# Early loads of a one-core SSM and linear-attention kernel: decay vectors at the head of GpSimd's queue, x in pairs ahead of B

## The chip, the cores and the metric

One core of one Trainium2 chip. The metric is the device time of one execution of the whole program in microseconds. The core has five engines with a queue each: TensorE (PE: matrix products, with weight loads PEld beside them), VectorE (DVE), ScalarE (ACT), GpSimd (POOL) and SyncE (SP), which here only issues DMAs.

## The reference, cut to what matters

The input x has 2048 rows of 512. Two branches read it, and a gate per row mixes them.

```python
g = sigmoid((x * gate_w).sum(-1, keepdims=True))
# a: diagonal state space model
Lam_bar = exp(exp(log_dt) * (Lambda_re + 1j * Lambda_im))
Bu = einsum("bld,pd->blp", x, ((Lam_bar - 1) / Lam)[:, None] * Bmat)
h_t = Lam_bar * h_(t-1) + Bu_t                      # 2048 steps
a = 2 * real(einsum("blp,dp->bld", h, Cmat)) + x * Dskip
# b: linear attention, 32 heads of 16
q, k, v = x @ wqkv
phi = concat(softmax(.. @ w_phi), softmax(-(.. @ w_phi)))   # of q and of k
b = (phi_q @ (phi_k^T v)) / (phi_q . sum phi_k + 1e-6) @ wo
out = g * a + (1 - g) * b
```

## The kernel before, in words

The rows of x are put into 16 tiles of 128 (tile `ti` holds every eighth row: residue `ti // 2`, half `ti % 2`), and each tile is loaded transposed, so that its 512 features lie along the partitions: `x_load(ti)`, a transposing DMA issued by SyncE into a slice of `xT` (L230). All products that read x use these tiles.

The work is cut into some 250 small generators (`st_...`), and a string `ORDER` written out by hand (L24 to L53) says in which order their steps are recorded. A token names a generator, and each time it stands there the generator goes one step on: the first step of `k3@5` records the four products of K for tile 3 into PSUM bank 5, the second `k3` records the cast that empties the bank. `:D` or `:A` picks VectorE or ScalarE for such a cast; `F:28` records 28 filler products that compute nothing. Each engine works through its own instructions strictly in the recorded order and waits on semaphores where another engine's or a DMA's result is needed. The hardware DMAs of SyncE and ScalarE share eight completion semaphores (lanes) in turn, and an issue waits until the transfer that used its lane before has landed.

The stages, in the order of TensorE:

- Fold: `W0..W3` transpose the K weights (`ptw`, L275), `f0..f3` multiply them with BD, a block diagonal of `w_phi` (`pf`, L432), and casts write `Wk2`. BD (L344) needs `mask16`, which VectorE reduces from an identity matrix that GpSimd makes (`make_identity`); the identity is also what TensorE transposes with.
- The three decay vectors go into `vec_n` by three small GpSimd DMAs (L252), `V` transposes them on TensorE (`pvt`, L311), and `P`, `P2`, `P3`, `P4`, `U`, `i0..i3` and `M` work out decay factors and tables on ScalarE, VectorE and GpSimd.
- `k0..k15` and `v0..v15` are the products of K and V of the 16 tiles (L476, names `pk` and `pv`). `x`, `n`, `e`, `s` make the softmax features of groups of tiles on VectorE and ScalarE (`EEk`; the last step, L549, scales them), and `a0..a4` sum features times V into `kvacc` (L579).
- `g..` are the products with B (`pgq`, L602), fed by `NR` and `NI`, which load both halves of B (`Bn`, L285), and `R0..R7`, which transpose it by DMA (L289). Later come the scan (`z`, `h`), the queries (`q`), and the outputs (`y`, `o`, `t`).

SyncE's queue before the change: `w_phi`, x tiles 0 to 3, the V weights `Wv` (L239), x tiles 4 to 7, then from `ORDER` both halves of B, seven of the x tiles 8 to 15 one by one (`l10 l13 l9 l12 l14 l11 l8`), `R0`, `R1`, `l15`, and further transposes.

Of the kernel before, what the change touches and what calls it, by code (L numbers as in the profile page):

```python
# [23 lines left out]
ORDER = """  # L24
NR F:28 NI B W1@0 W0@1 W0 W2@2 W1:D W3@3 W3 f1@4 W2:D f0@5 f2@6 f0 f1:D l10 V@0 F:4 V P f3@1 f3 f2:D F:4 P P k1@2 k1
l13 P2 k0@3 P2 U P2 P2 P2 P2 P4 k2@4 P3 P3 k3@5 P4 P4 k0 v0@0 i0 i2 U i0 i0 i1 i2 k4@7 i0:D i0 k2 i2 i2:D i2 U k3 k5@6
i1 v3@1 n0 x0 l9 i1 V2@2 i3 l12 x0 k4 v2@3 i3 i3 l14 i1 k5 n0 x0 n0 x0 i3 k7@4 n0 x0 U n0 i1 l11 k6@5 n1 x1 x1 n1 x1
n1 l8 R0 R1 x1 i3 k7 M v7@7 x1 n1 n1 k6:D L V2 v1@6 x2 n2 e0 v6@4 v5@5 v4@2 e0 x2 s0 v0 l15 n2 s0 n2 v2 s0 v1 R2 s0 v6
v3 n2 k10@0 k10 s0 k9@3 k9 C4 k13@6 gw D R3 s0 k12@4 e1 v7 s0 e1 s1 C6 k11@1 k11 x2 s1 k14@0 k8@3 k12 k14 k8 v4 k13
a0@71 a0 x2 s1 x2 s1 v5 g00@4 g00 g60@0 n2 x3 s1 g20@3 g60 s1 g10@2 g10 n3 e2 g30@6 g40@5 g10 s1 a1 x3 g20 n3 a1 x3 n3  # L30
x3 g41@4 n3 C3 e2 e2 e2 x3 g30 g40 g30 k15@0 k15 n3 e3 s2 x4 s2 x4 g01@2 g01 e3 e3 s2 g50@3 g11@5 g50 s2 s2 s2 n4 x4
n4 Q3 n4 s2 g50 g21@6 e3 s3 v8@0 g31@2 g11 Q2 g11 n4 g70@3 Q1 s3 C7 g21 g70 v9@5 g70 g70 z0 z0 g31 g31 Q0 w1@6 C0 a2
a2 a2 w0@3 s3 z0 v11@2 v9 g61@5 g41 R4 z0 w1 v8 z0 z0 g61 s3 w2@4 s3 s3 a2 x4 z0 z0 g51@6 g51 x4 w2 C2 s3 w3@0 g51 v11
n4 R5 w3 g71@5 g71 g71 g71 z1 z1 g02@4 g02 g42@6 a3 a3 z0 z0 g42 w0 e4 e4 z1 z1 z1 g62@2 g12@0 q1@5 C1 h50@4 C5 J1 e4
e4 z1 q2@6 q2 g12 g12 g22@3 g22 J0 h50 z1 z1 g62 q3@4 q3 J2 s4 z1 s4 q0@6 z1 s4 q0 q1 xA nA g32@0 J3 g32 g32 h60@3 J0
g52@2 g52 c4 h60 J2 c4 g52 h51@4 c2 s4 s4 g72@6 R7 g72 xA h10@5 nA g72 g72 c2 xA J3 nA h10 v10@0 v10 J1 s4 c5 h51 c5
R6 g23@3 v12@2 c4 c0 c0 g63@5 nA z2 z2 a3 a3 g03@4 xA g03 z2 z2 z2 z2 xA g23 z2 z2 g33@6 c5 v12 z2 z2 g13@0 g13 g63
g43@4 h32@3 g13 nA g43 h52@2 h52 g33 h32 h61@5 h61 h12@0 c0 g53@4 h12 g33 g53 s4 v14@3 c2 eA eA h42@2 h42 g73@6 g53 eA
eA g73 g73 q10@5 sA h11@0 h11 O h00@4 g73 sA v13@2 h00 v13 a4 z3 sA v15@6 z3 v15 h20@0 h01@4 h30@2 v14 h20 sA h30 z3
h31@6 z3 z3 sA a4 h01 h31 c6 c6 sA q13@3 q13 z3 a4 a4 Y Y h22@0 G q10 z3 z3 G q6@2 q6 h22 z3 z3 sA sA Y Y c1 c1 q9@4  # L40
q8@6 q5@7 h62@3 h41@5 c3 h41 c1 c3 c3 h13@0 h62 q11@2 h13 q11 q8 q12@1 c6 q12 h21@5 q5 h21 h02@2 c7 q4@6 q4 h53@3 h53
h23@1 h23 h33@0 h33 sA q9 h40@7 h40 sA q7@5 h43@6 h63@3 c7 h43 q7 c7 y4@0 y4 sA h63 sA h03@1 END h02 o0@4 o0 X1 N1
o1@7 o1 q14@6 X1 N1 h03 o0@5 X1 o1@2 o1 o1 o0 o0 q15@3 o2@4 o2 o2@7 o2 N1 q15 X1 N1 X1 N1 E1 E1 y2@1 y1@2 y1 E1 E1 q14
X2 y0@5 y0 o1 y4 X2 N2 X2 o0 o0 o3@4 o3 o3@7 o3 o1 o3 y2 X2 N2 o2 X2 N2 S1 S1 N2 S1 o3 S1 N2 S1 S1 o3 y5@3 o2 o2 S1 S1
S1 y1 E2 E2 E2 E2 y9@6 G N3 y5 y5 y3@4 y2 X3 X3 N3 t1 G t1 N3 S1 N3 S2 y9 y9 S2 S2 S1 S1 S2 y3 y3 t3 y0 t0 t0 t2 t2
y6@7 X3 t2:A o4@2 o4 o4@5 o4 o4 y6 y6 t3 X3 o4 X3 o4 S2 S2 t3 o5@1 o5 o5@2 o5 o5 y13@5 y13 o5 N3 o6@4 S2 o6 o6@1 o6 o6
y12@2 o5 y7@4 y7 y12 o6 o6 t4 y7 S2 S2 t4:D S2 E3 E3 E3 E3 S2 o7@1 o7 t5 t5 S3 o7@0 o7 S3 o7 t6 S3 o7 S2 o7 y8@1 o8@3
t6 o8 o8@0 o8 o8 S3 S3 y12 t0:A y11@7 o8 o8 o9@3 o9:D o9@0 o9:D S3 y8 y8 o9 o9 S3 S3 o9 o10@3 y11 o10 o10@0 y11 o10
o10 S3 y14@3 S3 y14 t7 t7:D t8 y14 t8 y15@0 o11@4 S3 o11 o11@1 t9 o12@4 o11:D o11 S3 o10 o10 o12 o12@1 o12 o12 t9:D
o11 y15 o13@4 o13:D o13@6 t6:A o13 o13 o11 o12 y10@1 o14@4 y15 o14:D o12@6 t9 o12:D t7:A t1 y10 y10 o13 o15@4 o15  # L50
o15@6 t4:A t5 o15 o15 t8 o15 t12 t12 t12:A t10 o14@4 o14 o14 t10:D o13@6 t11 o15@2 o15 t10 o13:D t11 t11:A y13 t13 o14
o14@1 t15 t13 t13 t15 t15 o14:D t14 t14 t14:A
"""  # L53
# [16 lines left out]
def kernel(  # L70
# [156 lines left out]
    x_res = x2.rearrange("(a c r) d -> r a c d", r=NR, c=P)

    def x_load(ti):
        nc.sync.dma_start_transpose(out=xT[:, :, ti * P:(ti + 1) * P], in_=x_res[ti // 2, ti % 2])  # L230
# [8 lines left out]
    nc.sync.dma_start(out=Wv[:], in_=B_wqkv[:, 2 * D:3 * D].rearrange("(k p) n -> p k n", p=P))  # L239
# [7 lines left out]
    tabp = tab_g.__enter__()  # L247
    iot = tabp.tile([P, NC], F32, name="iot", bufs=1)
    nc.gpsimd.iota(iot[:], pattern=[[1, NC]], base=0, channel_multiplier=0, allow_small_or_imprecise_dtypes=True)
    for t_, srcs in ((vec_n, (A_Lambda_im, A_Lambda_re, A_log_dt)), (vec_m, (A_Dskip, gate_w))):  # L250
        for n, src in enumerate(srcs):
            nc.gpsimd.dma_start(out=t_[4 * n:4 * n + 4, :], in_=src.rearrange("(j p) -> j p", p=P))  # L252
# [608 lines left out]
```

## Time and profile before

| | us |
|---|---|
| three runs | 155.34, 154.69, 155.97 (median 155.34) |
| the profiled execution | 155.2 |
| its span in the profile | 153.1 |
| TensorE busy | 147.5 (96%) |
| VectorE busy | 133.1 (87%) |
| ScalarE busy | 129.3 (84%) |
| GpSimd busy | 15.8 (10%) |
| mean granted clock of TensorE | 0.998 |

The span runs from the first to the last instruction of the program; the execution's own time is 2.1 us longer. In a row of the timeline the first number is the start, the second the length, then engine, line, operation, output<-inputs, and `x20` for twenty merged instructions; brackets hold the idle time before it and what ended it. `SPq` is the issue of a DMA, whose data lands later. A busy TensorE in these rows is not TensorE at its peak, since its products overlap: the distance from one start to the next tells the rate.

### The profile page before, as it was taken

The page shows a single profiled execution, that of the slowest core. Times are in us where ns is not written, and L with a number is a line of the kernel's source. Part 1 is how long each engine was busy: PE and PEld are TensorE (multiplying, and loading weights), DVE is VectorE, ACT ScalarE, POOL GpSimd, SP SyncE. Part 2 cuts the span into 40 slices and gives each one's busy share as a digit, 9 for nine tenths or more (in the row PEclk, how much of TensorE's full clock was granted, in tenths as well). Part 3 has the DMA queues.
Part 4 walks back from the last instruction along what each step waited for, and adds up shares of the span by engine and source line. Part 5 has one row for each costly group of instructions (what it writes and reads, how often), then busy time and mean ns, then how long its engine had stood idle before and what let it go on. Part 6 is the DMA issues. An engine that isn't in the chain of part 4 may idle for free.

```text
span 153.1 us, 3382 instructions
## 1 busy us (share of the span) xinstructions
PE 147.5 (96%) x1254; PEld 95.5 (62%) x1254; DVE 133.1 (87%) x304; ACT 129.3 (84%) x279; POOL 15.8 (10%) x43
## 2 busy tenths in 40 slices
PE   7999979999999999999999999999999999999990
PEld 7844434788878986869867656555555555546550
DVE  3799999999999999999999999999999858716441
ACT  3589998999998999999998999699488998618471
POOL 8239980000000000000000000000000000000000
PEclk9999999999999999999999999999999999999999
DMA  4785996494455699720000007911159959989943
GB/s 122 158 215 77 232 160 143 99 79 104 103 107 100 133 222 178 167 97 4 0 0 4 0 0 167 76 37 33 36 98 144 178 125 187 168 139 186 255 145 104
DMA packets 50992, 17.55 MB, mean 115 GB/s; under 512 B 44192, under 2 KB 50976, under 8 KB 50976
## 3 DMA queue, kind: packets, MB, share of 16 engines
q1 hardware_dynamic: 49120, 15.82, 57.0%
q10 hardware_dynamic: 1696, 1.51, 3.1%
q8 instruction: 10, 0.16, 0.5%
q0 software_dynamic: 160, 0.01, 0.2%
q14 instruction: 6, 0.05, 0.2%
HBM read 2.64 MB, written 2.10 MB: 31 GB/s over the span
## 4 chain that ended last, share of the span: by engine, by line
PE 80%; SPq 9%; DMA 8%; issue 1%; DVE 0%; ACT 0%
PE pgq L602 18%; PE py L718 16%; PE py L766 9%; PE pq L476 9%; SPq L230 7%; DMA xT<-in_A_x_dram 5%; PE pk L476 5%; PE pv L476 5%; PE ph L669 4%; DMA phT<-EEq 3%; PE kvacc L579 3%; PE pn L737 3%; PE pgq L607 2%; PE py L723 2%; PE pgq L609 2%; SPq L285 1%
## 5 line engine op out<-in xcount | busy, mean ns | idle before, releaser
L602 PE MATMUL pgq<-xT,BT 128*128 128x256 bf16 x256 | 31.5, 273 | 0.0
L476 PEld LDWEIGHTS <-xT 128*128 128x128 bf16 x192 | 18.1, 97 | 19.2 <-DMA xT<-in_A_x_dram 1.7
L602 PEld LDWEIGHTS <-BT 128*128 128x128 bf16 x256 | 24.6, 98 | 4.1
L139 ACT ACTIVATE EEk<-EEk 128x1024 bf16<-128x1024 bf16 x20 | 20.5, 1082 | 0.0
L120 ACT CAST uv<-pgq 128x512 bf16<-128x512 f32 x28 | 15.9, 605 | 0.7 <-PE pgq L602 0.5
L766 PE MATMUL py<-Wo,oT 128*128 128x512 bf16 x64 | 15.9, 380 | 0.0
L476 PE MATMUL pv<-Wv,xT 128*128 128x512 bf16 x64 | 15.8, 379 | 0.0
L476 PE MATMUL pq<-Wq,xT 128*128 128x512 bf16 x64 | 15.6, 379 | 0.0
L476 PE MATMUL pk<-Wk,xT 128*128 128x512 bf16 x64 | 14.8, 380 | 0.8 <-DMA xT<-in_A_x_dram 0.8
L139 ACT ACTIVATE EEq<-EEq 128x1024 bf16<-128x1024 bf16 x12 | 11.7, 1043 | 0.2 <-DVE EEq L528 0.2
L139 ACT ACTIVATE ld<-pn 128x16 f32<-128x16 f32 x32 | 6.1, 191 | 6.1 <-PE pn L737 4.7
L778 ACT ACTIVATE ot<-py,G 128x512 bf16<-128x512 f32 x11 | 7.4, 689 | 4.0 <-PE py L766 3.6
L591 ACT ACTIVATE phT<-X,dgB 128x512 bf16<-128x512 bf16 x16 | 10.7, 725 | 0.0
L120 ACT CAST nu<-pn 128x256 bf16<-128x256 f32 x27 | 9.9, 381 | 0.0
L745 DVE TENSOR_TENSOR on<-nu,rd 128x512 bf16<-128x512 bf16 x16 | 6.7, 421 | 3.5 <-ACT rd L139 1.8
L120 ACT CAST Xq<-pk 128x512 bf16<-128x512 f32 x15 | 8.6, 597 | 1.3 <-PE pk L476 1.3
L120 ACT CAST vx<-pv 128x512 bf16<-128x512 f32 x16 | 9.1, 603 | 0.4 <-PE pv L476 0.4
L549 DVE TENSOR_TENSOR EEk<-EEk,rck 128x4096 bf16<-128x4096 bf16 (+1 forms) x5 | 9.3, 1859 | 0.0
L120 ACT CAST Xq<-pq 128x512 bf16<-128x512 f32 x16 | 8.9, 609 | 0.2 <-PE pq L476 0.2
L766 PEld LDWEIGHTS <-oT 128*128 128x128 bf16 x64 | 5.5, 97 | 5.7 <-DMA oT<-on 0.8
L737 PEld LDWEIGHTS <-phT 128*128 128x128 bf16 x128 | 6.3, 97 | 3.5 <-DMA phT<-EEq 0.8
L512 DVE TENSOR_TENSOR smk<-smk 128x512 bf16<-128x512 bf16 (+4 forms) x18 | 8.1, 447 | 0.1
(180 smaller groups left out, 323.9 us busy)
## 6 DMA issues: line engine op xcount, KB each, us to landing
X<-HM SPq DMA_DIRECT2D x8, 256.0 KB, 4.4
out_dram<-ot SPq DMA_DIRECT2D x8, 128.0 KB, 2.2
out_dram<-ot ACTq DMA_DIRECT2D x7, 128.0 KB, 2.7
C2r<-in_B_wqkv_dram ACTq DMA_DIRECT2D x2, 256.0 KB, 3.5
Wv<-in_B_wqkv_dram SPq DMA_DIRECT2D x1, 512.0 KB, 4.1
Bn<-in_A_B_re_dram SPq DMA_DIRECT2D x1, 512.0 KB, 6.4
Bn<-in_A_B_im_dram SPq DMA_DIRECT2D x1, 512.0 KB, 7.2
Wo<-in_B_wo_dram SPq DMA_DIRECT2D x1, 512.0 KB, 4.1
```

What stands on the lines that cost most here:

```text
L120: nc.scalar.copy(out=out_ap, in_=in_ap)
L139: ins = nc.scalar.activation(**kw)
L230: nc.sync.dma_start_transpose(out=xT[:, :, ti * P:(ti + 1) * P], in_=x_res[ti // 2, ti % 2])
L476: MM(out=pt[:], lhsT=xT[:, kt, ti * P:(ti + 1) * P], rhs=W[:, kt, :], start=(kt == 0), stop=(kt == KT - 1))
L512: VT(out=dst, in0=cur[:, :, :, 0:n, :], in1=cur[:, :, :, n:2 * n, :], op=op)
L549: VT(out=E5, in0=E5, in1=rc.to_broadcast([P, L, 2 * NB, Dh, 4]), op=ALU.mult)
L591: nc.scalar.mul(out=t_, in_=x_, mul=c_)
L602: MM(out=pg[:, h, :], lhsT=BT[:, kt, 2 * j + h, :], rhs=xT[:, kt, r * NC:(r + 1) * NC], start=(h == 0 and kt == 0), stop=(r % 2 == 0 and k ...
L718: MM(out=py[:], lhsT=hs(r, t, slice(a * P, (a + 1) * P)), rhs=C2B[t], start=(t == 0), stop=False)
L737: MM(out=pn[:, 4 * m:4 * m + 4, :].rearrange("p h e -> p (h e)"), lhsT=ph[:, 4 * hf + m, :], rhs=KVm[:, 4 * hf + m, :], start=(m == 0), st ...
L766: MM(out=py[:], lhsT=oT[:, g, :], rhs=Wo[:, g, :], start=False, stop=(g == HG - 1))
L778: nc.scalar.mul(out=ot[:], in_=py[:], mul=G[:, ti:ti + 1])
```

## The change

Four things move; what is computed stays.

- The three GpSimd DMAs of the decay vectors are issued ahead of `make_identity`; those of Dskip and the gate stay behind it.
- `V` stands between the folds `f1` and `f0` instead of behind all but one; there are 34 fillers instead of 36.
- x tiles 0 and 1 are loaded singly, then `Wv`, then pairs of tiles in one transposing DMA each: 2-3, 4-5, 6-7 and 10-11, then both halves of B, then 8-9, 12-13, 14-15, and only then the transposes of B. Before, four single tiles stood ahead of `Wv`, four behind it, and eight behind B.
- The order of products begins `k0 k1 v0 k2 k3 k4 k5` instead of `k1 k0 k2 k3 v0 k4 k5`; the second half goes `k10 k11 k9 k12 k13 k14 k8` instead of `k10 k9 k13 k12 k11 k14 k8`.

```diff
-NR F:28 NI B W1@0 W0@1 W0 W2@2 W1:D W3@3 W3 f1@4 W2:D f0@5 f2@6 f0 f1:D l10 V@0 F:4 V P f3@1 f3 f2:D F:4 P P k1@2 k1
-l13 P2 k0@3 P2 U P2 P2 P2 P2 P4 k2@4 P3 P3 k3@5 P4 P4 k0 v0@0 i0 i2 U i0 i0 i1 i2 k4@7 i0:D i0 k2 i2 i2:D i2 U k3 k5@6
+l10 NR NI l8 l12 l14 F:28 B W1@0 W0@1 W0 W2@2 W1:D W3@3 W3 f1@4 W2:D V@0 f0@5 f2@6 V P f0 f1:D f3@1 P f3 F:6 f2:D P P2
+k0@2 P2 k0 P2 U k1@3 P2 P2 P2 P4 v0@0 k2@4 P3 P3 k3@5 P4 P4 k1 i0 i2 U i0 i0 i1 i2 k4@7 i0:D i0 k2 i2 i2:D i2 U k3
...
-    x_res = x2.rearrange("(a c r) d -> r a c d", r=NR, c=P)
-    def x_load(ti):
-        nc.sync.dma_start_transpose(out=xT[:, :, ti * P:(ti + 1) * P], in_=x_res[ti // 2, ti % 2])
+    x_res = x2.rearrange("(ac r) d -> r ac d", r=NR)
+    def x_load(ti, n=2):
+        a = ti % 2
+        nc.sync.dma_start_transpose(out=xT[:, :, ti * P:(ti + n) * P], in_=x_res[ti // 2, a * P:(a + n) * P])
+    def rows_in(t_, srcs):
+        for n, src in enumerate(srcs):
+            last_row = nc.gpsimd.dma_start(out=t_[4 * n:4 * n + 4, :], in_=src.rearrange("(j p) -> j p", p=P))
+        return last_row
+    rows_in(vec_n, (A_Lambda_im, A_Lambda_re, A_log_dt))
     make_identity(nc, ident[:])
...
-    for ti in range(4):
-        x_load(ti)
+    for ti in range(2):
+        x_load(ti, 1)
     nc.sync.dma_start(out=Wv[:], in_=B_wqkv[:, 2 * D:3 * D].rearrange("(k p) n -> p k n", p=P))
-    for ti in range(4, 8):
+    x_load(2)
+    for ti in (4, 6):
         x_load(ti)
...
-    for t_, srcs in ((vec_n, (A_Lambda_im, A_Lambda_re, A_log_dt)), (vec_m, (A_Dskip, gate_w))):
-        for n, src in enumerate(srcs):
-            nc.gpsimd.dma_start(out=t_[4 * n:4 * n + 4, :], in_=src.rearrange("(j p) -> j p", p=P))
+    rows_in(vec_m, (A_Dskip, gate_w))
```

More of the change, by code (lines that the diff above doesn't have):

```diff
@@ L30 @@
[L30 to L44, printed above, removed]
@@ new lines @@
+e3 s3 v8@0 g31@2 g11 Q2 g11 n4 g70@3 Q1 s3 C7 g21 g70 v9@5 g70 g70 z0 z0 g31 g31 Q0 w1@6 C0 a2 a2 a2 w0@3 s3 z0 v11@2
+v9 g61@5 g41 R4 z0 w1 v8 z0 z0 g61 s3 w2@4 s3 s3 a2 x4 z0 z0 g51@6 g51 x4 w2 C2 s3 w3@0 g51 v11 n4 R5 w3 g71@5 g71 g71
+g71 z1 z1 g02@4 g02 g42@6 a3 a3 z0 z0 g42 w0 e4 e4 z1 z1 z1 g62@2 g12@0 q1@5 C1 h50@4 C5 J1 e4 e4 z1 q2@6 q2 g12 g12
+g22@3 g22 J0 h50 z1 z1 g62 q3@4 q3 J2 s4 z1 s4 q0@6 z1 s4 q0 q1 xA nA g32@0 J3 g32 g32 h60@3 J0 g52@2 g52 c4 h60 J2 c4
+g52 h51@4 c2 s4 s4 g72@6 R7 g72 xA h10@5 nA g72 g72 c2 xA J3 nA h10 v10@0 v10 J1 s4 c5 h51 c5 R6 g23@3 v12@2 c4 c0 c0
@@ new lines @@
+g63@5 nA z2 z2 a3 a3 g03@4 xA g03 z2 z2 z2 z2 xA g23 z2 z2 g33@6 c5 v12 z2 z2 g13@0 g13 g63 g43@4 h32@3 g13 nA g43
+h52@2 h52 g33 h32 h61@5 h61 h12@0 c0 g53@4 h12 g33 g53 s4 v14@3 c2 eA eA h42@2 h42 g73@6 g53 eA eA g73 g73 q10@5 sA
+h11@0 h11 O h00@4 g73 sA v13@2 h00 v13 a4 z3 sA v15@6 z3 v15 h20@0 h01@4 h30@2 v14 h20 sA h30 z3 h31@6 z3 z3 sA a4 h01
+h31 c6 c6 sA q13@3 q13 z3 a4 a4 Y Y h22@0 G q10 z3 z3 G q6@2 q6 h22 z3 z3 sA sA Y Y c1 c1 q9@4 q8@6 q5@7 h62@3 h41@5
+c3 h41 c1 c3 c3 h13@0 h62 q11@2 h13 q11 q8 q12@1 c6 q12 h21@5 q5 h21 h02@2 c7 q4@6 q4 h53@3 h53 h23@1 h23 h33@0 h33 sA
@@ new lines @@
+q9 h40@7 h40 sA q7@5 h43@6 h63@3 c7 h43 q7 c7 y4@0 y4 sA h63 sA h03@1 END h02 o0@4 o0 X1 N1 o1@7 o1 q14@6 X1 N1 h03
+o0@5 X1 o1@2 o1 o1 o0 o0 q15@3 o2@4 o2 o2@7 o2 N1 q15 X1 N1 X1 N1 E1 E1 y2@1 y1@2 y1 E1 E1 q14 X2 y0@5 y0 o1 y4 X2 N2
+X2 o0 o0 o3@4 o3 o3@7 o3 o1 o3 y2 X2 N2 o2 X2 N2 S1 S1 N2 S1 o3 S1 N2 S1 S1 o3 y5@3 o2 o2 S1 S1 S1 y1 E2 E2 E2 E2 y9@6
+G N3 y5 y5 y3@4 y2 X3 X3 N3 t1 G t1 N3 S1 N3 S2 y9 y9 S2 S2 S1 S1 S2 y3 y3 t3 y0 t0 t0 t2 t2 y6@7 X3 t2:A o4@2 o4 o4@5
+o4 o4 y6 y6 t3 X3 o4 X3 o4 S2 S2 t3 o5@1 o5 o5@2 o5 o5 y13@5 y13 o5 N3 o6@4 S2 o6 o6@1 o6 o6 y12@2 o5 y7@4 y7 y12 o6
@@ new lines @@
+o6 t4 y7 S2 S2 t4:D S2 E3 E3 E3 E3 S2 o7@1 o7 t5 t5 S3 o7@0 o7 S3 o7 t6 S3 o7 S2 o7 y8@1 o8@3 t6 o8 o8@0 o8 o8 S3 S3
+y12 t0:A y11@7 o8 o8 o9@3 o9:D o9@0 o9:D S3 y8 y8 o9 o9 S3 S3 o9 o10@3 y11 o10 o10@0 y11 o10 o10 S3 y14@3 S3 y14 t7
+t7:D t8 y14 t8 y15@0 o11@4 S3 o11 o11@1 t9 o12@4 o11:D o11 S3 o10 o10 o12 o12@1 o12 o12 t9:D o11 y15 o13@4 o13:D o13@6
+t6:A o13 o13 o11 o12 y10@1 o14@4 y15 o14:D o12@6 t9 o12:D t7:A t1 y10 y10 o13 o15@4 o15 o15@6 t4:A t5 o15 o15 t8 o15
+t12 t12 t12:A t10 o14@4 o14 o14 t10:D o13@6 t11 o15@2 o15 t10 o13:D t11 t11:A y13 t13 o14 o14@1 t15 t13 t13 t15 t15
@@ L53 @@
+o14:D t14 t14 t14:A
 """
```

16 lines of the change are left out of this document (5 added, 11 removed).

## The prediction

> **What bounds the kernel now.** I read the page first, then the busy time by stretches, then the chain of waits, then TensorE's timeline around the one place where the chain leaves TensorE.
>
> ```profile
> span 153.1 us, 3382 instructions
> PE 147.5 (96%) x1254; PEld 95.5 (62%) x1254; DVE 133.1 (87%) x304; ACT 129.3 (84%) x279; POOL 15.8 (10%) x43
> ```
>
> ```profile
> 22.00:30.00 8.00, 7.64 (x59) 4.06 (x60) 7.93 (x19) 7.14 (x15) 0.51 (x1) 1.00 0.64 131
> 30.00:45.00 15.00, 15.00 (x148) 12.62 (x147) 14.93 (x26) 14.97 (x27) 0.00 (x0) 1.00 0.62 98
> 45.00:60.00 15.00, 15.00 (x184) 12.30 (x183) 14.91 (x32) 14.30 (x29) 0.00 (x0) 1.00 0.84 159
> ```
>
> The columns of the second view are the stretch, its length, then the busy time of TensorE, its weight loads, VectorE, ScalarE and GpSimd, the granted clock and DMA. VectorE is full from 22 us on (7.93 of 8, then 14.9 of 15), TensorE from 30 us; between 22 and 30 us TensorE alone has a hole. Where both are full, time given to one of them alone is worth only what the other can follow.
>
> ```profile
> 14.42 7.89 DMA xT<-in_A_x_dram
> ...
> 57.12 0.86 PE pq L476 x4
> ```
>
> ```profile
> 17.06 4.49 PE L476 MATMUL pv<-Wv,xT 128*128 128x512 bf16 x20
> 22.36 6.34 PE L476 MATMUL pk<-Wk,xT 128*128 128x512 bf16 x28 [0.80 <-DMA xT<-in_A_x_dram]
> 28.54 0.42 PE L579 MATMUL kvacc<-vx,EEk 128*128 128x68 bf16 x8
> ...
> 34.71 0.42 PE L579 MATMUL kvacc<-vx,EEk 128*128 128x68 bf16 x8
> ```
>
> The chain of waits shows one transfer of x, issued at 14.42 us and landing 7.89 us later at 22.31; TensorE goes on 0.05 us behind it. Unstalled, four 512-column products take 0.86 us (0.215 each). Twenty from 17.06 would end at 21.36, and the next starts at 22.36: a stall of 1.0 us. The 28 products from 22.36 should take 6.02 us, and the following group starts 6.18 us later, so 0.15 us more is lost, again to x. That is the whole early stall: 1.15 us.
>
> **What the change does, part by part.**
>
> **x in pairs, ahead of B.** SyncE issues these one after the other:
>
> ```profile
> 1.31 5.21 SPq L230 DMA_TRANSPOSE xT<-in_A_x_dram  x4
> 6.57 0.59 SPq L239 DMA_DIRECT2D Wv<-in_B_wqkv_dram  x1
> ...
> 12.37 1.34 SPq L285 DMA_DIRECT2D Bn<-in_A_B_re_dram  x1
> 13.75 0.62 SPq L285 DMA_DIRECT2D Bn<-in_A_B_im_dram  x1
> ```
>
> A single tile costs 5.21/4 = 1.3 us of the queue. A pair moves twice the data; no such transfer of x is in the trace. The nearest row is the transpose into phT, [128, 8, 128] against [128, 4, 128] for a tile of x, so just as much data as a pair (its source is SBUF, not HBM):
>
> ```profile
> L564 SPq DMA_TRANSPOSE phT<-EEq x12: 1247/1292/2247, 113.1 to 138.7; - x12
> ```
>
> Its median issue, 1.29 us, is that of half the data. I take 1.3 us for a pair; the upper end is twice a tile, 2.6, the lower the 1.25 us of phT's fastest. With 1.3 the queue runs: tiles 0 and 1 at 1.31 and 2.65, Wv at 3.94, pair 2-3 at 4.58, 4-5 at 5.9, 6-7 at 7.2, 10-11 at 8.5, the two halves of B at 9.8 and 11.1, then 8-9 at 11.8, 12-13 at 13.1, 14-15 at 14.4. The lane waits before these issues are for transfers landed by then. Seven issues fewer take some 9 us off the queue, and the first transpose of B goes out when B has landed, by 19.0 us if its second half takes the 7.89 us of the tile behind it today; the last tiles of x no longer stand in front of it.
>
> [...]
>
> Landing, from issue, by the page's last column:
>
> ```profile
> Wv<-in_B_wqkv_dram SPq DMA_DIRECT2D x1, 512.0 KB, 4.1
> ...
> xT<-in_A_x_dram SPq DMA_TRANSPOSE x16, 3.9
> oT<-on SPq DMA_TRANSPOSE x12, 2.7
> phT<-EEq SPq DMA_TRANSPOSE x12, 3.3
> ```
>
> So Wv lands at 8.0. A tile of x takes 3.9 us, and a pair adds the 0.6 us by which phT, twice the data, takes longer than oT: pair 2-3, issued at 4.58, lands at 9.1. The far bound is the tile behind B, 7.89 us, hence 12.5. The order of products becomes k0, k1, v0, k2: with 0.86 us a tile from 7.4, k2 starts at 10.0. It is met by 0.9 us. Pair 4-5, 1.3 us behind, has until 11.7; 6-7 until 15. Tile 10 is wanted at 21.4 and tile 9 at 23.1, both over 3 us behind their landing even with B's 7 us counted. The 1.15 us stall goes: **-1.15 us** on TensorE.
>
> V of tile 0 ahead of k2 is a change of order among equal products (0.86 each): nothing by itself. It gives pair 2-3 that time, and if Wv were later than 9.1 it would cost what it is late.
>
> **Vectors first on GpSimd.** Three issues now stand ahead of the identity, which VectorE needs for the mask of the fold operand BD.
>
> ```profile
> 0.79 0.20 POOL masks.py:197 MEMSET ident<- 128x128 bf16 x1 [0.29 <-POOLq L845]
> ...
> 1.42 0.28 POOL masks.py:199 TENSOR_SCALAR_AFFINE_SELECT identf<-identf 128x128 f32<-128x128 f32 x1
> ...
> 1.96 0.77 POOL L252 DMA_DIRECT2D vec_n<-in_A_Lambda_im_dram  x1
> 2.74 0.52 POOL L252 DMA_DIRECT2D vec_n<-in_A_Lambda_re_dram  x1
> 3.26 0.52 POOL L252 DMA_DIRECT2D vec_n<-in_A_log_dt_dram  x1
> ```
>
> ```profile
> 2.75 0.06 DVE L257 MEMSET eps_p<- 64x1 f32 x1
> 4.06 0.69 DVE L344 TENSOR_TENSOR BD<-Wc,mask 128x512 bf16<-128x512 bf16 x1 [1.25 <-DMA Wc<-in_B_w_phi_dram]
> 4.90 0.42 DVE L122 COPY Xq<-ptw 128x512 bf16<-128x512 bf16 x1
> ```
>
> They take 0.77 + 0.52 + 0.52 = 1.81 us, so the float identity is done at 1.70 + 1.81 = 3.51. Behind it on VectorE stand the two reductions, maskN and the eps memsets, which end 1.11 us after it today (2.81): now 4.62. BD follows at 4.65 instead of 4.06, and the copy of W1 behind it ends at 4.65 + 0.69 + 0.42 = 5.76 or a little more. The first fold starts today at 5.78:
>
> ```profile
> 5.78 0.85 PE L432 MATMUL pf<-BD,Xq 128*128 128x128 bf16 x12
> 6.56 0.18 PE L311 MATMUL pvt<-ident,vec_n 12*128 12x12 bf16 x1
> ```
>
> With 0.05 us from an end to TensorE's start it goes at 5.83 to 5.87: **+0.05 to +0.09 us**. The cover is the 1.25 us that BD now waits for Wc, and the wait of W1's copy for its transposes. BD later than about 4.6 costs one for one. The bound upward is all three issues at 0.77: BD at 5.15, +0.55.
>
> **V between the folds.** V ran at 6.56, so the vectors had landed by then; issued 1.17 us earlier (0.79 against 1.96) they land by 5.4, before f1 ends at about 6.05. V (0.18) now stands ahead of f0, f2 and f3 on TensorE, its cast ahead of f1's on VectorE, the exponential ahead of f0's cast on ScalarE.
>
> ```profile
> 7.01 0.21 ACT L139 ACTIVATE ssm_par<-vec 128x4 f32<-128x4 f32 x1
> ```
>
> The same small instructions run as before, and two filler products fewer; what follows on VectorE starts about 0.09 us late at most, and k0 at 7.4 instead of 7.35. I put this inside the +0.09. Its bounds are -0.14 (two fillers saved, 0.07 each as the fold's products, 0.85 for 12) and +0.21 (the exponential, put in front of a cast that k0 needs).
>
> **Where the stall goes.** TensorE comes 1.06 us earlier to the first sums of K and V, at 27.5 instead of 28.54. They read the features that VectorE finishes here:
>
> ```profile
> 26.68 1.22 DVE L549 TENSOR_TENSOR EEk<-EEk,rck 128x2048 bf16<-128x2048 bf16 x1
> ...
> 33.03 1.22 DVE L549 TENSOR_TENSOR EEk<-EEk,rck 128x2048 bf16<-128x2048 bf16 x1
> ```
>
> VectorE is full up to there, and nothing in its work is taken away. It ends the first group at 27.90, the second at 34.25. TensorE waits at the first until 27.96 (0.58 of the gain is left), and at the second until 34.31 against 34.71: 0.40 is left, less VectorE's own 0.09. Behind that both run in step to 115 us, so what is left reaches the end.
>
> **The sum:** -1.15 + 0.09 + 0.48 (wait at the first sums) + 0.27 (at the second) = **-0.3 us**. The profiled execution took 155.2 us, 2.1 outside its span; that gives 154.9. The median of the three runs is 155.34, which gives 155.0. I forecast **155.0**: 0.2% less.
>
> **The rivals.**
>
> *VectorE follows.* If the work of VectorE also moved up, the full 1.06 to 1.15 would stay: 154.1. For it: x and the vectors are earlier. Against: VectorE's queue has no idle time up to 27.9 that an earlier input could fill.
>
> *A pair behind Wv lands late (slower).* If pair 2-3 needs the 7.89 us of the tile behind B, it lands at 12.5 and k2 waits 2.5 us. Of that 1.06 is the stall removed later; +1.4 stays: 156.6. It turns from gain to loss where the pair lands after 11.1, so over 6.5 us. For it: twice the data behind 512 KB. Against: the median tile takes 3.9 us with the same transfers about it.
>
> *GpSimd keeps the identity back.* With all issues at 0.77, +0.55 instead of +0.09: 155.4. It decides from BD at about 4.9. For it: the first issue took 0.77. Against: the other four took 0.52.
>
> [...]
>
> **Chances.** Forecast 0.50, VectorE follows 0.12, late pair 0.13, late identity 0.15, dear issue 0.10. The range of 154.1 to 156.6 reaches from the second to most of the late pair. A measurement of this kernel can tell about 1% (1.55 us) from no change. No case gains that; with the spread of the runs (154.69 to 155.97) I leave 0.07 for faster. Slower by it needs the late pair beyond its row, or two mishaps: 0.14. The rest, 0.79, is within 1%.
>
> **What would show it.** Right: no wait of TensorE for x at 21 to 24 us; pair rows of about 1.3 us on SyncE; BD near 4.65 and the first fold near 5.85; a new wait of the K and V sums at 28.0 and 34.3 for VectorE's features; the end 0.3 us earlier. Wrong: k2 waiting for x at 10 us, pair issues near 2.6 us, a first fold beyond 6.0, or K and V sums at 27.5 without a wait.

## The result, and the profile after

| | before | after |
|---|---|---|
| median of 22 executions each (us) | 154.87 (154.47 to 155.97) | 155.54 (154.98 to 157.72) |
| ratio, 95% interval | | 1.0048 [1.0024, 1.0071] |
| the profiled execution, its span | 155.2, 153.1 | 157.17, 155.2 |

The forecast of 155.0 stood for 0.2% less; the change costs 0.5%. The time lies in the stated range and within 1%, but the change went the other way. The spans of the changed kernel fall into two groups: 16 of the 22 lie between 153.1 and 154.1 us, four between 154.8 and 155.2 (the profiled one among them); the last two (155.4 and 155.5) took over 1.5% longer than the shortest, and such executions are left out of the ratio, here and below, but not of the median.

TensorE's timeline after, with the rows that answer to the stall and to the first sums:

```profile
6.08 0.40 PE L438 MATMUL pf<-BD,Xq 128*128 128x128 bf16 x4
6.42 0.18 PE L317 MATMUL pvt<-ident,vec_n 12*128 12x12 bf16 x1
...
7.60 1.77 PE L482 MATMUL pk<-Wk,xT 128*128 128x512 bf16 x7
...
17.40 4.57 PE L482 MATMUL pv<-Wv,xT 128*128 128x512 bf16 x20
21.80 6.21 PE L482 MATMUL pk<-Wk,xT 128*128 128x512 bf16 x28
28.30 0.43 PE L585 MATMUL kvacc<-vx,EEk 128*128 128x68 bf16 x8 [0.29 <-DVE EEk L555]
...
34.60 0.43 PE L585 MATMUL kvacc<-vx,EEk 128*128 128x68 bf16 x8
```

The wait for x ahead of the 28 products is gone; they start at 21.80 instead of 22.36. But the first fold starts at 6.08 (before 5.78), k0 at 7.60 (before 7.35), and at the first sums of K and V TensorE waits for VectorE until 28.30 (before: no wait, 28.54).

The start, on GpSimd and VectorE (two answers of the timeline):

```profile
1.32 0.78 POOL L235 DMA_DIRECT2D vec_n<-in_A_Lambda_im_dram  x1 [0.82 <-POOLq L851]
...
3.75 0.30 POOL masks.py:199 TENSOR_SCALAR_AFFINE_SELECT identf<-identf 128x128 f32<-128x128 f32 x1
```

```profile
4.08 0.29 DVE L243 TENSOR_REDUCE mask<-identf 128x8 bf16<-128x128 f32 x1 [1.91 <-POOL identf masks.py:199]
...
5.00 0.69 DVE L350 TENSOR_TENSOR BD<-Wc,mask 128x512 bf16<-128x512 bf16 x1
```

The float identity is done at 4.05, VectorE waits 1.91 us for it, and BD starts at 5.00 instead of 4.06.

SyncE further on. Its first transposes of the output stage (oT, phT) come behind all the work of K, V, scan and queries, and so mark what the first two thirds have cost. Before:

```profile
105.36 7.68 SPq L759 DMA_TRANSPOSE oT<-on  x4
113.15 6.49 SPq L564 DMA_TRANSPOSE phT<-EEq  x4
```

After:

```profile
105.35 7.67 SPq L765 DMA_TRANSPOSE oT<-on  x4
113.14 6.57 SPq L570 DMA_TRANSPOSE phT<-EEq  x4
```

At 105 us these two executions are 0.01 us apart: of the stall of 1.15 us nothing is left. A second profiled execution of the changed kernel (`after_again` below) has this row at 105.12, with the same start of k0, so one such row is good to about 0.2 us. Whatever makes this execution slower than the one before lies behind 113 us. There its chain of waits shows a transpose that lands 5.64 us behind its issue:

```profile
130.56 5.64 DMA oT<-on
136.20 0.05 issue
136.25 1.90 PE py L772 x8
```

The waits of TensorE from 113 to 150 us list it (the kernel before has none there):

```profile
PE py L772 <- DMA oT<-on: 1.5, 2, 1.4
PE pn L743 <- DMA phT<-EEq: 0.3, 1, 0.3
```

Last, the end of the program. The instructions of the last line are not work but waits and drains; SyncE waits there for every DMA lane (by the trace seven of the nine waits name the semaphores of all eight lanes). Before (the last output is issued by L784 at 150.57 and lands 1.65 us later, at 152.22):

```profile
L856 SPq EVENT_SEMAPHORE  x9: 17/28/28, 151.0 to 153.1; - x9
...
L856 SPq DRAIN  x3: 7/7/13, 152.3 to 152.6; - x3
```

After (issued at 152.30, landed at 153.96):

```profile
L862 SPq EVENT_SEMAPHORE  x9: 17/28/1304, 152.7 to 155.2; - x9
...
L862 SPq DRAIN  x3: 7/7/13, 154.4 to 154.7; - x3
```

The three numbers are the shortest, median and longest in ns. Before, no wait is longer than 28 ns, and the drain follows 0.1 us behind the landing. After, one wait takes 1304 ns, and it is the first: from 152.7 to 154.0, when the last output lands. The others still stand behind it, and the drain comes 0.4 us behind the landing. From the last landing to the end of the span it is 0.92 us before and 1.28 us after.

### The profile page after: what moved, and what is told of

It reads as the page before. It is cut to its first block, busy times and chain, and to the rows that moved or that the text cites. A ratio compares the mean times of both kernels' runs of the same rounds, so it can differ in the third digit from the quotient of the medians.

```text
span 155.2 us, 3371 instructions
## 1 busy us (share of the span) xinstructions
PE 148.0 (95%) x1252; PEld 95.6 (62%) x1252; DVE 132.7 (85%) x304; ACT 129.1 (83%) x279; POOL 13.0 (8%) x43
## 5 line engine op out<-in xcount | busy, mean ns | idle before, releaser
L784 ACT ACTIVATE ot<-py,G 128x512 bf16<-128x512 f32 x11 | 7.4, 689 | 5.2 <-PE py L772 4.7
```

The costliest lines, as they stand in the source:

```text
L784: nc.scalar.mul(out=ot[:], in_=py[:], mul=G[:, ti:ti + 1])
```

## The experiments

Every kernel but one (`after_again`, a single execution) was timed in 6 to 12 executions beside the kernel before on the same chip, and the ratio is to those. The series ran on several chips, on which the kernel before itself had medians of 154.87 to 155.57 us; the changed kernel has a full series in the first of them alone.

### The parts

*x loads alone* (`x_only`):

```diff
 (to the changed kernel)
-    rows_in(vec_n, (A_Lambda_im, A_Lambda_re, A_log_dt))     # ahead of the identity
+    rows_in(vec_n, (A_Lambda_im, A_Lambda_re, A_log_dt))     # behind iota
-... V@0 f0@5 f2@6 V P f0 f1:D f3@1 P f3 F:6 f2:D P P2
+... f0@5 f2@6 f0 f1:D V@0 F:4 V P f3@1 f3 f2:D F:4 P P P2
```

> The change with the GpSimd order, V's place and the 36 fillers as before: only the loads of x and B and the order of products move. Theory 1 (start): the early issues on GpSimd keep the identity back and put VectorE's whole queue 0.3 us late, which uses up the gain of the x loads; without them the first sums of K and V start at 28.0 us (before 28.54, changed 28.30), the second at 34.35 (34.71, 34.60), and TensorE is 0.3 us ahead of before from there to the first transpose of an output near 105 us. Theory 2 (end): the loss lies behind 113 us, in transposes that land late while 16 KB of instructions are fetched; then the 0.3 us are seen at 105 us all the same, and the time is 154.5 us where the end goes as before, up to 155.2 where it does not. Rival: the loads of x themselves cost the 0.6 us; then 155.4 us or more.

Measured: 155.27 us against 155.29, ratio 1.0007 [0.9977, 1.0036]. Its TensorE and its SyncE:

```profile
7.33 1.89 PE L482 MATMUL pk<-Wk,xT 128*128 128x512 bf16 x7
...
21.38 6.21 PE L482 MATMUL pk<-Wk,xT 128*128 128x512 bf16 x28
27.94 0.43 PE L585 MATMUL kvacc<-vx,EEk 128*128 128x68 bf16 x8 [0.36 <-DVE EEk L555]
```

```profile
104.96 2.50 SPq L765 DMA_TRANSPOSE oT<-on  x2
```

With k0 where it was before, the x loads bring 0.40 us to 105 us in this execution, about what the prediction left of the stall at the second sums; the median does not show it.

*Vectors and V alone* (`vec_only`): the kernel before, with the vectors first and V between the folds.

> Before, with the three decay vectors first on GpSimd, V between the folds and 34 fillers; x as before. Theory 1: BD at 5.0 us and the first fold at 6.08 as in the changed kernel, VectorE 0.3 us late, which still fits into the slack of 0.58 and 0.40 us that the sums of K and V have behind the stall on x: first sums at 28.54 us, second at 34.7, time within 0.1 us of before (154.9). Rival: the vectors' part alone makes the 0.6 us: 155.5 us. Theory 2 says no sign for this kernel, only that a difference of more than 0.2 us lies behind 113 us.

Measured: 155.97 us, ratio 1.005 [1.002, 1.008]. k0 starts at 7.73, but the first transpose of the output stage stands at 105.36, exactly as before:

```profile
105.36 2.50 SPq L763 DMA_TRANSPOSE oT<-on  x2
```

With the old loads the late fold costs nothing up to there: it falls into the stall on x. So the two parts do not add up: the stall was the cover of the late fold. In this execution (155.51 us, one of the shorter ones) the loss lies behind 105 us; where the longer ones lose their time was not profiled.

### The start: queue of GpSimd, or landing of the vectors

*Vectors behind the identities, V between the folds* (`mid`):

```diff
 (to the changed kernel)
-    rows_in(vec_n, (A_Lambda_im, A_Lambda_re, A_log_dt))
     make_identity(nc, ident[:])
     identf = stg.tile([P, P], F32, name="identf", bufs=1)
     make_identity(nc, identf[:])
+    rows_in(vec_n, (A_Lambda_im, A_Lambda_re, A_log_dt))
```

> The changed kernel, but the three vector issues stand behind both identities on GpSimd (ahead of iota), with V still between the folds. Theory of the start: the changed kernel's BD starts at 5.00 us only because the three issues keep the identity back; here BD is back at 3.9 to 4.1 us, the first fold at 5.8, the first cast of a fold at 6.2 and not 6.72, and VectorE's full queue is 0.3 to 0.4 us earlier from there on, so that the first transpose of the output stage is issued at 104.9 to 105.0 us, as with the x loads alone (104.96), and not at 105.35. Rival: V between the folds costs it (its cast and the exponential in front of the folds' casts), then it stays at 105.3. For the end: with the start 0.4 us earlier the median would be 154.5; if the stretch behind 113 us gives its own 0.4 us and more whatever the start does, as it did with the x loads alone, it is 155.0 to 155.4.

Measured: 156.82 us, ratio 1.0086 [1.0053, 1.0119]. BD was back at 3.88 us, and it was of no use:

```profile
6.89 0.16 PE L317 MATMUL pvt<-ident,vec_n 12*128 12x12 bf16 x1 [0.49 <-DMA vec_n<-in_A_log_dt_dram]
...
8.06 1.99 PE L482 MATMUL pk<-Wk,xT 128*128 128x512 bf16 x7
```

V waits for the third vector, which lands at 6.76, and three folds stand behind V. My theory of the start (BD alone) fell here.

*Vectors issued by ScalarE* (`act_96`): `nc.scalar` instead of `nc.gpsimd` for the three, the output weights in five pieces.

> The changed kernel with the three vectors issued by ScalarE behind its two weight loads instead of by GpSimd, and the output weights in five pieces (96 issues). Theory of the start: the identity is done at 1.7 us again, BD at 3.9 to 4.1, V between the folds without a wait if the vectors land by 6.2 (issued at 1.9 to 3.4, landing 3 to 3.5 us behind), k0 at 7.2 to 7.4 and the first transpose of the output stage at 104.8 to 105.0. Rival: the vectors still land behind 6.2 (they wait for the weights' and x's data, not for their queue), V waits between the folds and k0 comes at 7.5 to 8 and that landmark at 105.2 to 105.6.

Measured: 157.33 us, ratio 1.0105 [1.0056, 1.0153]. ScalarE's queue:

```profile
1.93 0.58 ACTq L235 DMA_DIRECT2D vec_n<-in_A_Lambda_im_dram  x1
4.09 0.26 ACTq L235 DMA_DIRECT2D vec_n<-in_A_Lambda_re_dram  x1
```

The second issue comes 1.6 us behind the end of the first: by the trace it has the lane of the first weight load, and waits for that transfer's semaphore. V runs at 7.70. The rival had the direction (V waits), but not the wait on the lane, and not the size: k0 starts at 9.69 instead of 7.5 to 8, and the first transpose of the output stage stands at 107.11. Behind V the same twelve fold products take 1.46 us that take 0.84 in the changed kernel:

```profile
7.70 0.17 PE L319 MATMUL pvt<-ident,vec_n 12*128 12x12 bf16 x1 [1.92 <-issue]
7.80 1.46 PE L440 MATMUL pf<-BD,Xq 128*128 128x128 bf16 x12
```

```profile
8.00:10.00 2.00, 2.00 (x19) 0.50 1.14 228
```

The second view gives the stretch, its length, TensorE's busy time, the granted clock and DMA: after the 1.92 us without work TensorE was granted half its clock, from 7.3 to 10.8 us by the trace. In the changed kernel it is 1.00 in these stretches. In four of this kernel's six executions the mean granted clock is 0.985 to 0.989, against 0.994 or more in every execution of the changed kernel.

*Float identity first, then the vectors, then the other identity* (`idf_96`, with 96 DMA issues, see below):

> The changed kernel with 96 DMA issues (output weights in eight pieces), and on GpSimd the float identity first, then the three vectors, then the other identity. Theory of the start: with the float identity done by about 2.3 us VectorE's mask work runs ahead of Wc again and BD starts at 3.9 to 4.1 us; if the vectors still land by 6.3 us (in the changed kernel 5.7 to 6.4), V between the folds does not wait, k0 comes at 7.3 to 7.4 instead of 7.6 and the median is 155.0 to 155.2, 0.2 to 0.4 us under the kernel before. Rival: the vectors, a few tenths later, land behind 6.4 us in most executions, V waits, and what BD gains is lost there: 155.5 as with 96 issues alone.

Measured: 155.48 us against 155.55, ratio 0.9996 [0.9969, 1.0023]. BD starts at 3.99, and again V waits (third vector landed at 6.67, k0 at 7.97):

```profile
6.81 0.16 PE L319 MATMUL pvt<-ident,vec_n 12*128 12x12 bf16 x1 [0.58 <-DMA vec_n<-in_A_log_dt_dram]
```

Both conditions must hold at once: BD early and the vectors landed by 6.2 (an estimate, from the first fold at 5.8 us in the kernel before and the 0.39 us that four of its products take). One profiled execution has both, that of `mid_fill14` below (BD at 3.96, the third vector landed at 6.05, V without a wait): k0 starts at 7.50 and the first transpose of the output stage stands at 105.25, still behind `x_only`. In the profiled executions with GpSimd's issues the third vector landed between 5.7 and 8.2 us. What a late k0 costs shows in the kernels with x in pairs:

| kernel | k0 starts | first transpose of the output stage | difference |
|---|---|---|---|
| `x_only` | 7.33 | 104.96 | 97.63 |
| after | 7.60 | 105.35 | 97.75 |
| `after_96` | 7.69 | 105.41 | 97.72 |
| `idf_96` | 7.97 | 105.70 | 97.73 |
| `x_96` | 7.99 | 105.63 | 97.64 |
| `mid` | 8.06 | 105.79 | 97.73 |
| `pair01` | 9.14 | 106.70 | 97.56 |
| before (x singly) | 7.35 | 105.36 | 98.01 |

Over 1.8 us of k0 the difference stays within 0.19 in these rows with x in pairs, and the eight other executions with pairs lie between 97.4 and 97.8: from k0 on there is no cover left, and what k0 is late is late at 105 us, to within 0.3 us. With x singly it is another matter. `vec_only`, `before_fill14` and `before_issue97` have k0 at 7.73, 7.78 and 7.59 and that transpose at 105.36, 105.45 and 105.16, about where the kernel before has it. So the stall covered some 0.4 us of a late k0.

### The end: the lane of the last output

The changed kernel has seven hardware DMA issues fewer (x in 9 instead of 16): 89 instead of 96 by the trace. By the trace they use eight semaphores (lanes) in turn, so 96 end on the last lane of the round and 89 on the first: the last output has semaphore 109, the eighth of the round, before, and 107, the first, after.

*One issue more* (`before_issue97`): the kernel before, output weights in two halves.

```diff
-        nc.sync.dma_start(out=Wo[:], in_=B_wo.rearrange("(k p) n -> p k n", p=P))
+        wo_ = B_wo.rearrange("(k p) n -> p k n", p=P)
+        for h_ in range(2):
+            nc.sync.dma_start(out=Wo[:, 2 * h_:2 * h_ + 2, :], in_=wo_[:, 2 * h_:2 * h_ + 2, :])
```

> The kernel before, with the load of the output weights written as two halves: one DMA issue more (97), nothing else. Theory of the lanes: the last output's lane becomes the first of the final order, the time from its landing to the end of the program is 1.28 us instead of 0.92, the median 155.3 + 0.36 = 155.6 to 155.7. Rival: no difference at the end (0.92 us), 155.3.

Measured: 155.83 us against 155.38, ratio 1.0023 [0.9993, 1.0052]. The final waits:

```profile
L858 SPq EVENT_SEMAPHORE  x9: 17/28/1293, 150.6 to 153.1; - x9
```

One more issue makes the long first wait, with 1.29 us from the last landing (151.91) to the end. The median moves by 0.45, a little more than expected (0.3 to 0.4), though the interval of the ratio just reaches no change.

*One issue fewer* (`after_pair01`: tiles 0 and 1 in one pair, 88 issues):

```diff
-    for ti in range(2):
-        x_load(ti, 1)
+    x_load(0)
```

> The changed kernel with tiles 0 and 1 in one pair: 88 issues. Theory of the lanes: 0.92 us from the last landing to the end instead of 1.28; the start as in the changed kernel (BD at 5.0, k0 at 7.5 to 7.9, first transpose of the output stage at 105.3 to 105.5); the median 0.36 under that of the changed kernel, 155.2. Rival: as the changed kernel, 155.5.

Measured: 155.12 us against 155.38, ratio 1.0000 [0.9966, 1.0034]. The profiled execution is by far the longest (span 156.3, the other eleven 152.9 to 154.0): TensorE waits 1.36 us for K weights there, and has half its clock from 7.6 to 11.0 us. So only the final waits are read from it, none over 28 ns:

```profile
L861 SPq EVENT_SEMAPHORE  x9: 17/28/28, 154.1 to 156.2; - x9
```

*The same with the x loads alone* (`pair01`):

> The x loads of the change alone (GpSimd order, place of V and fillers as before), with tiles 0 and 1 also in one pair: 88 DMA issues by SyncE and ScalarE instead of 89 (before: 96). Theory of the lanes: at the end SyncE waits for the eight lanes in a fixed order, 0.065 us each; with 96 issues the last output stands on the last lane of that order, with 89 on the first, so that six waits follow its landing (+0.36 us from last landing to the end: 1.28 instead of 0.92 us). With 88 it is on the last again: 0.92 us. First transpose of the output stage at 104.9 to 105.0 (pair 0-1 lands by 6 us, k0 wants it at 7.33). Median 0.3 to 0.4 us under the x loads alone (155.27), so 154.9, unless the transposes behind 113 us land otherwise. Rival: the last 0.36 us has another cause and stays; or pair 0-1 lands after 7.33 and k0 waits.

Measured: 156.46 us, ratio 1.0074 [1.004, 1.0109]. The end is as expected (0.91 us from landing to end), the start is not: the 512 KB of Wv now leave at 2.71 us, the third vector lands at 8.23, and V, behind three folds, waits:

```profile
8.36 0.16 PE L316 MATMUL pvt<-ident,vec_n 12*128 12x12 bf16 x1 [1.46 <-DMA vec_n<-in_A_log_dt_dram]
```

*The changed kernel with 96 issues* (`after_96`: output weights in eight pieces, nothing else):

```diff
-        nc.sync.dma_start(out=Wo[:], in_=B_wo.rearrange("(k p) n -> p k n", p=P))
+        wo_ = B_wo.rearrange("(k p) n -> p k n", p=P)
+        for k_, h_, m_ in [(k_, h_, D // 2) for k_ in range(4) for h_ in range(2)]:
+            nc.sync.dma_start(out=Wo[:, k_, h_ * m_:h_ * m_ + m_], in_=wo_[:, k_, h_ * m_:h_ * m_ + m_])
```

> The changed kernel, with the load of the output weights written in eight pieces: 96 DMA issues by SyncE and ScalarE as before the change, instead of 89; nothing at the start or in the stages differs. Theory of the lanes: 0.92 us from the last landing to the end instead of 1.28, the lower group of spans at 153.0 instead of 153.4, the median 155.2 instead of 155.54. Rival: the rotation of the lanes costs nothing by itself, 155.5.

Measured: 155.47 us against 155.57, ratio 0.9991 [0.9964, 1.0017]. Beside the kernel before on this chip there is no loss; the interval lies below that of the change (1.0024 to 1.0071). The changed kernel itself was run on this chip only once (`after_again`, 156.87 us). Final waits and TensorE's waits from 113 to 150 us:

```profile
L864 SPq EVENT_SEMAPHORE  x9: 17/28/28, 151.4 to 153.5; - x9
```

```profile
PE pn L745 <- DMA phT<-EEq: 0.4, 1, 0.4
```

All its spans lie between 153.0 and 153.8: the upper group is gone as well, which I had not expected of the lanes. It isn't the chip that lacks it, since 5 of the 23 executions of the kernel before there have spans of 154.2 to 155.1.

The 0.36 us at the end do not rest on these runs alone. In all 19 profiled executions the time from the last landing to the end is 0.91 to 0.92 us with 88 or 96 issues and 1.27 to 1.28 us with 89 or 97.

*x loads alone with 96 issues* (`x_96`):

> The x loads of the change alone (GpSimd order, V and fillers as before), with the output weights in eight pieces: 96 issues. Start: k0 at 7.3 to 7.4 and the first transpose of the output stage at 104.9 to 105.0 as with the x loads alone; end: 0.92 us behind the last landing. Together 0.4 us less than before at the start and none lost at the end: 154.8 to 155.0, lower group of spans at 152.4 to 152.7, and faster than both kernels if the transposes of 131 to 136 us do not land late more often. Rival: the late transposes give all of it back, 155.3.

Measured: 156.03 us against 155.57, ratio 1.0008 [0.9974, 1.0041]: not faster. Here the third vector landed at 6.73 and k0 started at 7.99, and TensorE waited 0.7 us for an oT at 136 us. The 104.96 of `x_only` was one execution with early vectors (the third landed at 5.96).

### Behind 113 us: transposes that land late

A fetch of 16 KB of TensorE's instructions (`q8` below; that they are TensorE's is read from the runs of this part, in which it moves with their count) comes every 13 to 21 us there. In the kernel before there are ten in the span, and from the first (12.33 us) to the last (146.65 us) TensorE starts some 2300 products and weight loads, 256 from one fetch to the next on the mean. The DMA of the changed kernel from 132.6 to 134.6 us, in 40 slices:

```profile
DMA  9999766309000000999999000011000000000000
...
q14 instruction: 1, 0.01, 6.0%
q8 instruction: 1, 0.02, 3.8%
```

Two fetches begin in this window, 16 KB at 132.69 (1.23 us) and 8 KB at 133.09 (1.9 us), and for most of its second half the engines move next to nothing. The phT issued at 129.12 and the oT issued at 130.56, both unfinished, land at 135.98 and 136.20. In `after_96` the fetch begins at 132.89; there phT has landed at 132.49, and that oT lands at 133.36. Tenths of a us decide what is caught.

The 19 profiled executions agree on this. From 104 us on, 36 transposes into phT had a fetch of 16 KB begin during their first 3.3 us; they took 3.85 to 6.3 us to land, 4.8 in the median. The 149 that met no fetch took 3.3 us in the median (3.1 to 4.4). For oT (the first 2.5 us) it is 4.1 us (37 transposes) against 2.5 (141).

The count of TensorE's instructions was changed with nothing else, through the filler products at the start. *28 fewer* (`before_fill14`, `after_fill14`, `mid_fill14`):

```diff
-            for _ in range(int(eng)):
-                MM(out=spin[:, 0:P], lhsT=fillw[:], rhs=fillw[:], start=True, stop=True)
+            m_, n_ = (14, 2 * P) if eng == "28" else (int(eng), P)
+            for _ in range(m_):
+                MM(out=spin[:, 0:n_], lhsT=fillw[:, 0:P], rhs=fillw[:, 0:n_], start=True, stop=True)
```

> The kernel before with the 28 opening fillers made into 14 of twice the columns, 28 instructions fewer in TensorE's stream. Theory 2: the end of this kernel too moves with the place of the fetches, by 0.3 us or more, up or down, while TensorE's work up to 113 us keeps its times within 0.1 us. Rival: 154.9 us as before.

> The changed kernel with the 28 opening fillers made into 14 of twice the columns: the same time at the start, 28 instructions fewer in TensorE's stream, so that every later fetch of its instructions comes some 1.8 us later against the work (one row moves by 28 instructions of 256). Theory 2: the late landings of the transposes into phT and oT (6.87 and 5.64 us near 130 us in the changed kernel) move or go, and the median moves by 0.3 us or more, most likely down to 155.0. Rival (the end is slow for another reason): median 155.5 as in the changed kernel, and the same transposes late.

> The same as the run with the vectors behind the identities, with the 28 opening fillers written as 14 of 256 columns: 28 instructions fewer on TensorE, the same time at the start. Theory of the end: where the fetches of instructions fall among the transposes behind 113 us decides by some 1 us; 28 instructions fewer moved the changed kernel by +0.9 us (155.54 to 156.51) and the one before by +0.4 at most, so here again a shift between -0.5 and +1.0 us, with the landmarks at 105 and 113 us within 0.15 us of those of the kernel without it. Rival (the fetches do nothing): within 0.2 us of it at the end too.

Measured: 155.29 us, ratio 1.0027 [0.9998, 1.0055]; 156.51 us, ratio 1.01 [1.0071, 1.0129]; 156.7 us, ratio 1.0083 [1.0054, 1.0113]. The fetch of 114 to 117 us moved to 118.8 to 119.0. Now the third and fourth phT of the stage at 113 us took 4.9 to 5.4 us to land, and the first two 3.2 to 3.4 instead of 4.2 to 4.9; the later fetch hardly moved (132.6 to 133.9). So the late landings follow the fetch, but the medians answer only in part: the kernel before stays where it is (155.29 beside 155.29) and `mid` too (156.82 to 156.7), as the rival said, though TensorE's longest wait for an oT went from 0.2 to 1.3 us there while k0 came 0.56 us earlier. The changed kernel stands 0.5% higher than in its own series (ratio 1.01 against 1.0048, on another chip), in part because the vectors landed late in it (V waited 0.28 us in its profile).

*56 more* (`after_p56`, `mid_p56`):

```diff
+            m_, n_ = (56, 64) if eng == "28" else (int(eng), P)
+            for _ in range(m_):
+                MM(out=spin[0:n_, 0:n_], lhsT=fillw[:, 0:n_], rhs=fillw[:, 0:n_], start=True, stop=True)
```

> The changed kernel with the 28 opening fillers as 56 of 64 columns, so that the start is that of the changed kernel (BD at 5.0, first transpose of the output stage at 105.35) and only the place of TensorE's instruction fetches differs. Theory of the end: a different median from 155.54 by 0.3 us or more, either way, with all of the difference behind 113 us; 154.9 if the fetch at 133 us no longer falls among the transposes. Rival (all of the loss is in the start): 155.5.

> The same as the run with the vectors behind the identities, with the 28 opening fillers written as 56 of 64 weight columns and 64 moving columns: 56 TensorE instructions more, and the opening 3.2 us as long or shorter. Theory of the end: the fetches fall some 3 us earlier in the work (256 instructions take 15 to 16 us there), the fetch that comes at 132.7 us in the changed kernel comes at about 129 to 130, no longer within 0.5 us of the fetch on the other instruction queue at 133.1, and the transposes issued at 129 to 131 us land in 3.3 to 4.5 us instead of 5.6 to 6.9; median 154.4 to 154.8. Rival: the same end as without.

Measured: 156.88 us, ratio 1.0107 [1.0068, 1.0145], and 156.36 us, ratio 1.0085 [1.0052, 1.0117]. The first transpose of the output stage stands at 105.33 and 105.34, as in the changed kernel. The fetch came at 130.0 and 130.1, as expected, but not to any good: it caught the two phT of 127.3 and 128.7 (5.2 and 6.2 us to landing), while the oT of 132.8 landed in 2.8 us. TensorE's waits of `after_p56` there:

```profile
PE pn L743 <- DMA phT<-EEq: 1.2, 1, 1.2
PE py L772 <- DMA oT<-on: 0.7, 1, 0.7
```

In the changed kernel the stall moved with the fetch, from the oT of 136 us to the phT ahead of it, and kept its size (1.9 us in all, 1.8 before). `mid_p56` has the same wait of 1.2 us for phT, where `mid` had 0.4. The hope of a harmless place was not met.

*42 fewer, in `pair01`* (`pair01_m42`): 156.46 became 157.1, ratio 1.0113 [1.0063, 1.0162] against 1.0074 [1.004, 1.0109], so the two are not told apart.

> The x loads alone with all tiles in pairs, and the 28 opening fillers as 7 of 512 columns: 42 TensorE instructions fewer. Theory of the fetches: the one of 132 to 133 us falls 1 to 3 us later in the work; the loss at 131 to 136 us changes its size or its place, as it did with 56 more (then the transposes of 127 to 129 us came late by 2 us and the ones of 131 to 133 in time). If it falls behind 135 us, where the transposes are not wanted so soon, the median is 154.3 to 154.6; else within 0.5 us of the run without it. Rival: the fetches have nothing to do with it: the same landings as without.

The fetch of 133.7 moved to 135.1, still among the transposes.

*The changed kernel again, one execution* (`after_again`): 156.87 us, span 154.8.

> The changed kernel once more for a profile of the lower of its two groups of spans (153.1 to 154.1 in 16 of 22 executions; the profile at hand, 155.2, is of the upper). Theory of the end: in an execution of the lower group the transposes issued at 129 to 131 us land in 3.3 to 4.5 us and TensorE has no wait over 0.5 us there, while the first transpose of the output stage at 105.3 and the 1.28 us behind the last landing are as in the profile at hand. Rival: the difference of the groups lies ahead of 105 us (k0 late by the vectors), then that landmark is at least 1 us earlier.

This execution, too, was of the upper group, so the direct comparison is missing. It repeats the stall, with the first transpose of the output stage at 105.12 us:

```profile
PE py L772 <- DMA oT<-on: 1.6, 1, 1.6
```

That the upper group is this stall (1.5 us, against 1.4 us between the groups) is therefore argued from two executions that have it and from `after_96`, which has neither; no execution of the lower group was profiled. `x_only` agrees (its profiled execution, span 154.6, is of an upper group of four and waits 1.3 us there). Not every long span is this stall, though: `mid` has 154.8 with waits of 0.4 us and less, by a late k0 and several small waits.

## Why the prediction was wrong, point by point

Two steps failed. "Vectors first on GpSimd" was put at +0.05 to +0.09 us and measured +0.25 at k0, which took all of the 0.3 us that the sum had left in one profiled execution and a part of it in the other. And "what is left reaches the end" put everything behind 105 us at nothing, where the runs show +0.36 us at the last waits and, in some executions, 1.4 us of late transposes.

- *The stall of x, -1.15 us.* Right. It is gone (the 28 products follow the 20 by 4.40 us instead of 5.30), and x arrives in time everywhere.
- *Pair issue and landing.* Right in what mattered. Four of the seven pair issues take 1.23 to 1.31 us (forecast 1.3). The other three take 2.0, 2.4 and 4.1 us, although the transfers on their lanes had landed; what held them is open, and TensorE waited for none of them. Pair 2-3 lands at 9.12 (forecast 9.1); to hit it so closely is luck, since the seven pairs take 3.5 to 7.7 us from issue to landing. No run shows the dear issue (2.6 us for a pair, given 0.10 in the chances) as a matter of size: a pair takes as long as a single tile (1.31 us in the median of the seven, against 1.27 for the sixteen single tiles before), and in the kernel before phT takes 1.29 us in the median against 1.21 for oT, with twice the data. The late pair did not come either.
- *Vectors first on GpSimd, +0.05 to +0.09 us.* The size failed. I started the three issues where the first memset stood (0.79 us); the first issue only begins at 1.32. The identity was done at 4.05 instead of 3.51, BD at 5.00 instead of 4.65, k0 at 7.60 instead of 7.40. The lengths of the issues were right (0.78, 0.52 and 0.52 us). BD passed the 4.9 that I had given as the rival's point; its price at k0 was +0.25, not +0.55.
- *V between the folds, inside +0.09, bounds -0.14 to +0.21.* The step failed. I had the vectors landed by 5.4 us, from an issue 1.17 us earlier. The third was issued only 0.65 us earlier (2.61 against 3.26) and landed at 5.88 in the profile (before 6.43), at 6.64 in `after_fill14`, and once V is ahead of three folds, a late vector is a late k0. The bounds should have come from the landing, not from the instructions: `mid` shows k0 at 8.06.
- *The cap by VectorE.* The mechanism was right: TensorE waits at the first sums for VectorE's features, as forecast. The size was off by VectorE's own delay: 28.30 instead of 28.0, 34.60 instead of 34.31. With k0 undisturbed (`x_only`) the wait ends at 27.94 and 0.40 us reach 105 us.
- *"What is left reaches the end."* This failed twice. At 105 us 0.01 us was left in one profiled execution and 0.24 in the other, instead of 0.31; and I had not looked at the end of the program at all. Seven issues fewer put the last output on the lane that SyncE waits for first: +0.36 us. Add the four of twenty executions with some 1.4 us of late transposes, 0.28 us on the mean: 0.64 together, against 0.74 between the means of the executions compared (0.67 between the medians). The second term is the argued one.
- *Rivals.* "GpSimd keeps the identity back" came nearest in time (155.4 forecast), and its condition was met (BD at 5.00), but it explains only what is lost up to 105 us. Undoing the rotation alone (`after_96`) brings 0.9991 with BD still at 5.00; undoing the start alone (`x_only`) brings 1.0007 with the rotation left in. Either covers the loss, so neither is the whole cause. "VectorE follows" was wrong.

What stays open: whether and why 96 issues also thin out the late transposes (with 89 issues TensorE waits 1.3 to 1.6 us for an oT or phT there in the profiles of `x_only`, after, `after_again` and `mid_fill14`, 1.2 in the two `p56` and 0.8 in `after_fill14`, though only 0.4 in `mid`; with 96 or 97 at most 0.7; with 88 it is 1.4 in the long execution of `after_pair01`, and that kernel's other eleven spans have no upper group), how far the chip decides it (the kernel before has spans of 154.2 us and more in 5 of 23 and 6 of 29 executions on two chips, and in one at most of each other series), and where vectors and V alone lose their 0.5%. No version was found that beats both kernels: `after_96`, `after_pair01` and `idf_96` are equal to the kernel before.

## What to carry to other kernels

A stall on one engine can be the cover of another part of the same change (here the stall of 1.15 us covered some 0.4 us of a late k0); price each part with the other already done. Put no instruction that waits for a small, late DMA ahead of work that is ready, and take the landing's spread over several executions as its bound (here 5.7 to 8.2 us for the third vector). A wait put in front of that work can cost more than its length: in `act_96` the granted clock was 0.50 for some 3.5 us behind 1.92 us without work. When the number of DMA issues changes, look at what depends on their count: the lanes, an issue's wait for its lane (1.6 us in `act_96`), and the waits at the end (0.36 us here).
